# Split-precision chunked scan and expert layer: the first sweep's second product in fp32 from unsplit operands, and a first tile with masked logs

## The chip, the cores and the metric

One core of one Trainium2 chip runs the whole program. The metric is the device time of one execution in microseconds (us). In the profile PE is the matrix engine TensorE (PEld is its weight load), DVE is VectorE, ACT is ScalarE, POOL is GpSimd and SP is SyncE, which issues the DMAs.

## The reference

Two stages follow each other. The first is a scan with decay over 4 batches, 8 heads and 768 positions, head size 32 and state size 16; the second is a dense layer 256 to 2048 to 256 with `h - tanh(h)` between its two products.

```
log_a = log(clip(a, 1e-6, 1))
for each chunk:
    cum = cumsum(log_a in the chunk)
    L = exp(cum[i] - cum[j]) for i >= j, else 0
    y_intra = ((C @ B.T) * L) @ x
    y_inter = (C @ state) * exp(cum)
    state = exp(cum[-1]) * state + sum_j B[j] x[j] exp(cum[-1] - cum[j])
h = y @ w_in
g = h - tanh(h)
out = g @ w_out
```

## The kernel before

Tokens lie along the free axis, features along the partitions. The scan is done in 28 chunks of up to 112 positions (`Q = 112`, 7 chunks per batch); a state of 16 rows is carried in front of each chunk, so that a chunk has 128 rows. The dense layer works on 8 tiles of tokens, four of 256 tokens and four of 512 (`WIDTH`). The first four tiles are swept together: each of four sweeps takes four of the 16 blocks of the hidden layer (`SWEEPS`) through those four tiles, so that the weights, which arrive from memory meanwhile, are needed piece by piece. The last four tiles each take all 16 blocks at once.

Both products of the dense layer are done in split precision. A number is stored as a high and a low part in the type fp32r, and a product is three matmuls (high by high, high by low, low by high). So the weights are converted when they arrive (`conv`, L290 to L337: ACT and DVE rebuild fp32 from the 64-bit words in `raw`, ACT casts the high part `wh` at L321, DVE subtracts for the low part `wl` at L324), the scan's output is split into `xh` (ACT, L569) and `xl` (DVE, L572), and the hidden layer into `gh` (ACT, L651) and `gl` (DVE, L657). `mm1` (L629) is the first product, into `ph`; `act` applies tanh on ACT (L643) and subtracts on DVE (L647), into `g`; `mm2` (L683) is the second product, into `o`. In the narrow tiles one step of `mm1` or `mm2` covers two blocks of the hidden layer: 12 products of 128x128 by 128x256.

A chunk of the scan runs as a chain over the engines. For the first tile (chunks 0 to 2, `first_tile`, L378) PE forms the running sums of the logs in two halves of four heads each (`cp`, fp32, L387), ACT takes exp of one head at a time with a bias (`lt`, L404), PE forms C by B (`att`, L397), DVE multiplies (L409), POOL sets what lies above the diagonal to zero (L414), and PE multiplies by x (`y`, L541). For chunks 3 to 9 (`chunk_a`, L438) the difference of the sums comes out of one bf16 matmul of 9 rows (L451, from `lt_c` and `rt_c`, small tables that are sent through device memory as `cum3`), ACT does one exp of all heads (L460), DVE the product (L464), POOL the mask (L476). From chunk 10 on (`chunk_l`, L479) the sums arrive broadcast by a DMA from `cumr`. Chunk 10 is the first whose state is carried within the 128 rows: its `y` at L541 has the shape 128x128, once in the first sweep, and serves below as a mark in the trace. `z` (L553) is the state for the next chunk in chunks 0 to 4, in a place of its own; ACT copies it into the next `x` (L566).

The order of all instructions is made ahead of the run by a list scheduler in the program (`Order`, L52 to L218). Each operation is handed over with its engine and a cost in us; the scheduler tries 16 rounds of priorities from a random seed and keeps the best by its own costs. The engines then run their instructions strictly in that order, each with its semaphore waits. So any change of a cost, a table or the seed moves instructions on all engines.

## Time and profile before

| what | value |
|---|---|
| median of 3 runs | 337.64 us (335.47 to 447.55) |
| the profiled execution | 337.02 us |
| its span, first to last instruction | 335.1 us |
| PE busy | 321.2 us, 96% of the span |
| PE weight load | 269.7 us, 80% |
| DVE busy | 226.3 us, 68% |
| ACT busy | 218.3 us, 65% |
| POOL busy | 57.0 us, 17% |
| moved by DMA | 32.16 MB, mean 96 GB/s |

The time of the profiled execution is 1.9 us longer than its span: that part lies before the first and behind the last instruction. Busy shares are means over stages that differ; the stage that the change touches is the first fifth of the span. A matmul in fp32 is recorded as two instructions, one in fp32r or bf16 as one.

### The profile page before, as it was taken

The page shows a single profiled execution, that of the slowest core. Times are in us where ns is not written, and L with a number is a line of the kernel's source. Part 1 is how long each engine was busy: PE and PEld are TensorE (multiplying, and loading weights), DVE is VectorE, ACT ScalarE, POOL GpSimd, SP SyncE. Part 2 cuts the span into 40 slices and gives each one's busy share as a digit, 9 for nine tenths or more (in the row PEclk, how much of TensorE's full clock was granted, in tenths as well). Part 3 has the DMA queues.
Part 4 walks back from the last instruction along what each step waited for, and adds up shares of the span by engine and source line. Part 5 has one row for each costly group of instructions (what it writes and reads, how often), then busy time and mean ns, then how long its engine had stood idle before and what let it go on. Part 6 is the DMA issues. An engine that isn't in the chain of part 4 may idle for free.

```text
span 335.1 us, 6403 instructions
## 1 busy us (share of the span) xinstructions
PE 321.2 (96%) x2452; PEld 269.7 (80%) x2452; DVE 226.3 (68%) x346; ACT 218.3 (65%) x524; POOL 57.0 (17%) x77
## 2 busy tenths in 40 slices
PE   8867989899999999999999999999999999999995
PEld 7656878899999999877877777877787778888884
DVE  5898999999888855764556656456655554545552
ACT  7868889797666635856778783676676664544441
POOL 7445463121000200301111101121011010000000
PEclk9967999999999999999999999999999999999999
DMA  7759885280000006622432033323010000100001
GB/s 219 233 183 344 234 299 161 88 298 3 0 2 2 1 33 220 209 87 86 139 121 94 32 117 99 121 94 115 13 63 2 1 0 2 63 0 2 0 0 63
DMA packets 14441, 32.16 MB, mean 96 GB/s; under 512 B 2500, under 2 KB 5452, under 8 KB 14412
## 3 DMA queue, kind: packets, MB, share of 16 engines
q1 hardware_dynamic: 14412, 31.77, 28.4%
q8 instruction: 19, 0.31, 0.4%
q14 instruction: 10, 0.08, 0.1%
HBM read 28.33 MB, written 3.43 MB: 95 GB/s over the span
## 4 chain that ended last, share of the span: by engine, by line
PE 82%; DMA 8%; DVE 4%; ACT 2%; SPq 1%; issue 1%; POOL 0%; POOLq 0%
PE o L683 39%; PE ph L629 38%; DMA raw<-w_d 5%; PE y L541 3%; PE att L528 2%; DMA bc<-bc_d 2%; DMA braw<-bn_d 1%; ACT wv L300 1%; ACT lt L404 1%; DVE gl L657 1%; ACT x L566 0%; SPq L871 0%; DVE g L647 0%; DVE wm L305 0%; DVE xl L572 0%
## 5 line engine op out<-in xcount | busy, mean ns | idle before, releaser
L647 DVE TENSOR_TENSOR g<-ph,g 128x512 f32<-128x512 f32 x96 | 66.0, 689 | 67.6 <-ACT g L643 67.4
L643 ACT ACTIVATE g<-ph 128x512 f32<-128x512 f32 x96 | 57.2, 597 | 67.6 <-PE ph L629 65.9
L629 PE MATMUL ph<-xh,wh 128*128 128x256 f32 (+1 forms) x256 | 85.8, 346 | 0.0
L629 PE MATMUL ph<-xh,wl 128*128 128x256 f32 (+1 forms) x256 | 84.6, 341 | 0.0
L657 DVE TENSOR_TENSOR gl<-g,gh 128x512 fp32r<-128x512 f32 x96 | 68.8, 716 | 20.0 <-ACT gh L651 18.9
L651 ACT CAST gh<-g 128x512 fp32r<-128x512 f32 x96 | 59.5, 620 | 26.4 <-DVE g L647 25.4
L683 PE MATMUL o<-gh,wh 128*128 128x256 f32 (+1 forms) x256 | 72.2, 343 | 0.1
L683 PE MATMUL o<-gh,wl 128*128 128x256 f32 (+1 forms) x256 | 71.2, 339 | 0.0
L683 PE MATMUL o<-gl,wh 128*128 128x256 f32 (+1 forms) x256 | 70.8, 338 | 0.0
L629 PE MATMUL ph<-xl,wh 128*128 128x256 f32 (+1 forms) x256 | 65.8, 338 | 0.2 <-DVE xl L572 0.2
L476 POOL TENSOR_SCALAR_AFFINE_SELECT lt<-lt 128x896 f32<-128x896 f32 (+1 forms) x25 | 28.0, 1121 | 202.9 <-ACT lt L494 180.4
L629 PEld LDWEIGHTS ph<-xh,wh 128*128 128x128 f32 x256 | 49.2, 192 | 7.8 <-issue 1.6
L629 PEld LDWEIGHTS ph<-xh,wl 128*128 128x128 f32 x256 | 49.2, 192 | 5.3
L629 PEld LDWEIGHTS ph<-xl,wh 128*128 128x128 f32 x256 | 44.3, 191 | 6.0 <-DVE xl L572 0.4
L683 PEld LDWEIGHTS o<-gh,wh 128*128 128x128 f32 x256 | 41.5, 188 | 7.8 <-issue 1.9
L683 PEld LDWEIGHTS o<-gl,wh 128*128 128x128 f32 x256 | 41.6, 189 | 5.5
L683 PEld LDWEIGHTS o<-gh,wl 128*128 128x128 f32 x256 | 41.4, 188 | 5.2
L494 ACT ACTIVATE lt<-lt,ncum 128x112 f32<-128x112 f32 (+1 forms) x144 | 41.9, 377 | 0.0
L541 PE MATMUL y<-lt,x 128*32 128x128 f32 (+2 forms) x448 | 18.0, 275 | 6.4 <-ACT wh L321 3.1
L541 PEld LDWEIGHTS y<-lt,x 128*32 128x32 f32 x448 | 10.7, 110 | 14.0 <-issue 6.1
L532 DVE TENSOR_TENSOR lt<-att,lt 128x896 f32<-128x896 f32 (+1 forms) x18 | 19.0, 1058 | 0.0
L564 ACT COPY x<-s 16x64 f32<-16x64 f32 x60 | 14.4, 241 | 1.4 <-DVE s L559 0.7
(79 smaller groups left out, 229.8 us busy)
## 6 DMA issues: line engine op xcount, KB each, us to landing
lt<-cumr SPq DMA_DIRECT2D x18, 512.0 KB
raw<-w_d SPq DMA_DIRECT2D x16, 512.0 KB
bc<-bc_d SPq DMA_DIRECT2D x14, 352.0 KB
x<-x_d SPq DMA_DIRECT2D x14, 256.0 KB
out_d<-ob SPq DMA_DIRECT2D x8, 256.0 KB
braw<-bn_d SPq DMA_DIRECT2D x14, 112.0 KB
out_d<-ob SPq DMA_DIRECT2D x8, 128.0 KB
cum<-parts SPq DMA_DIRECT2D x1, 168.0 KB
```

What stands on the lines that cost most here:

```text
L476: nc.gpsimd.affine_select(out=k["l"][:, :, 0:q], in_=k["l"][:, :, 0:q], pattern=[[0, H], [1, q]], compare_op=ALU.is_ge, fill=0.0, base=N, ...
L494: nc.scalar.activation(k["l"][:, h, 0:q], k["l"][:, h, 0:q], AF.Exp, bias=ncum[:, h, ck : ck + 1])
L528: nc.tensor.matmul(out=a_[:, i], lhsT=bb[r], rhs=cc[r, :, 0 : qlen(ck + 1 + j)], start=True, stop=True)
L532: nc.vector.tensor_tensor(out=l, in0=chs[j]["a"], in1=l, op=ALU.mult)
L541: nc.tensor.matmul(out=y[r, hg * P : hg * P + P] if both else v[r, hg], lhsT=d["x"][:, cg, P * hg + D * h : P * hg + D * h + D], rhs=k["wh ...
L564: nc.scalar.copy(to.rearrange("p (g h d) -> p g h d", g=2, h=4)[:, :, i], k["s"][D * i : D * i + N])
L629: nc.tensor.matmul(out=ph[:, i * w : i * w + w], lhsT=w_[:, u, 0, k, j * P : (j + 1) * P], rhs=(xh, xl)[p][:, k, ts], start=p == 0 and k = ...
L643: nc.scalar.activation(g, gs[t, f][0], AF.Tanh)
L647: nc.vector.tensor_tensor(out=g, in0=ph, in1=g, op=ALU.subtract)
L651: nc.scalar.copy(gh, gs[t, f][1])
L657: nc.vector.tensor_tensor(out=gl, in0=g, in1=gh.bitcast(F32), op=ALU.subtract)
L683: nc.tensor.matmul(out=po[t, seg][e], lhsT=w_[:, u, 1, j, e * P : (e + 1) * P], rhs=g[:, i * w : i * w + w], start=f == seg[0] and k == 0 ...
```

## The change

Three parts, and with them a new order.

1. In the first sweep (tiles 0 to 3, blocks 0 to 3 of the hidden layer, eight steps of `mm2`) the second product takes `g` and the weights `wf` as they are, in fp32: four matmuls per step in the place of twelve. For these steps the parts `gh` and `gl` are not made. The output weights of the first two 512-row pieces are rebuilt into `wf`, and their split into `wh` and `wl` (`parted`) is moved behind, to just before tile 4 needs it. The second piece is converted in halves, as the first.
2. In the first tile POOL masks the logs ahead of the sums (`fn_k`), so that PE's sums come out as differences; PE adds a large negative number above the diagonal with one more bf16 matmul (`eye` by `never`), and ACT does one exp of 448 columns per half where it did four of 112. The mask behind the product is gone.
3. The fill of `rt_c` (`signs`) moves from POOL to DVE, the layout of `cum3` changes so that four loads of `rt_c` replace eight, and `cum3` is written by two DMAs where it was one. The scheduler's rate of DMA, its look-ahead, its seed and some costs are other numbers.

```diff
+NEVER = -2.0 ** 15
...
-APART, URGE = 5, 3.0
+APART, URGE, WHOLE = 5, 3.0, 2
...
-    DMA_LATENCY, SEM, SEM_PE, RATE, FLIGHT = 0.8, 0.15, 0.28, 0.24e6, 8
-    ROUNDS, JITTER, SEED, EARLY, LOOK = 16, 0.3, 69, 5.0, 0.35
+    DMA_LATENCY, SEM, SEM_PE, RATE, FLIGHT = 0.8, 0.15, 0.28, 0.32e6, 8
+    ROUNDS, JITTER, SEED, EARLY, LOOK = 16, 0.3, 174, 5.0, 0.5
...
+        def whole(s):
+            return u < WHOLE and s.start == 1
...
-            nc.vector.scalar_tensor_tensor(out=wv[u][:, s], in0=wv[u][:, s], scalar=0x80000000, in1=wm[u][:, s],
+            to = wv[u][:, s]
+            if whole(s):
+                to = wf[:, u : u + 1].bitcast(U32)
+            nc.vector.scalar_tensor_tensor(out=to, in0=wv[u][:, s], scalar=0x80000000, in1=wm[u][:, s],
                                            op0=ALU.bitwise_and, op1=ALU.bitwise_or)
...
+            if whole(s):
+                op("DVE", 1.2 * k, lambda s=s: fn4(s), r=[n_m[i], n_v[i]], w=[f"wf{u}"])
+                continue
...
+    def parted(u, after):
+
+        w_ = wf[:, u].rearrange("p (k c) -> p k c", k=2)
+        op("ACT", 0.62, lambda: nc.scalar.copy(wh[:, u, 1], w_), r=[f"wf{u}"], w=[f"wh{u}.1"], after=after)
+        op("DVE", 0.7, lambda: nc.vector.tensor_tensor(out=wl[:, u, 1], in0=w_, in1=wh[:, u, 1].bitcast(F32), op=ALU.subtract),
+           r=[f"wf{u}", f"wh{u}.1"], w=[f"wl{u}.1"])
...
+        def fn_k(ck, i):
+            chs[ck]["k", i] = p3.tile([P, BANK], F32, tag="g", name=f"lm{ck}_{i}").rearrange("p (h m) -> p h m", h=4)
+            nc.gpsimd.affine_select(out=chs[ck]["k", i], in_=la[:, 4 * i : 4 * i + 4, ck : ck + 1].broadcast_to([P, 4, P]),
+                                    pattern=[[0, 4], [-1, P]], compare_op=ALU.is_gt, fill=0.0, base=0, channel_multiplier=1)
+
         def fn_f(ck, i):
             f = chs[ck]["f", i] = ps_h.tile([P, 4, P], F32, tag="ph", name=f"cp{ck}_{i}")
+            nc.tensor.matmul(out=f[:, :, 0:Q], lhsT=eye, rhs=never.unsqueeze(1).broadcast_to([P, 4, Q]),
+                             start=True, stop=False, skip_group_check=True)
             for h in range(4):
-                nc.tensor.matmul(out=f[:, h, 0:Q], lhsT=la[:, 4 * i + h, ck : ck + 1].broadcast_to([P, P]),
-                                 rhs=upto[:, N:P], start=True, stop=True)
+                nc.tensor.matmul(out=f[:, h, 0:Q], lhsT=chs[ck]["k", i][:, h], rhs=upto[:, N:P], start=False, stop=h == 3,
+                                 skip_group_check=True)
...
-            for h in range(4):
-                nc.scalar.activation(chs[ck]["l"][:, 4 * i + h, :], chs[ck]["f", i][:, h, 0:Q], AF.Exp,
-                                     bias=ncum[:, 4 * i + h, ck : ck + 1])
+            nc.scalar.activation(chs[ck]["l"][:, 4 * i : 4 * i + 4], chs[ck]["f", i][:, :, 0:Q], AF.Exp)
...
-        def fn_s(ck, i):
-            lt = chs[ck]["l"][:, 4 * i : 4 * i + 4]
-            nc.gpsimd.affine_select(out=lt, in_=lt, pattern=[[0, 4], [1, Q]], compare_op=ALU.is_ge,
-                                    fill=0.0, base=N, channel_multiplier=-1)
...
-                n_f = slot("ph", NPH)
-                op("PE", 1.2, lambda ck=ck, i=i: fn_f(ck, i), r=["la", "upto"], w=[n_f])
-                op("ACT", 1.05, lambda ck=ck, i=i: fn_x(ck, i), r=[n_f, "ncum", "tab"], w=[k["n_l"][i]], urge=URGE)
+                n_f, n_k = slot("ph", NPH), slot("g", 3)
+                op("POOL", 0.7, lambda ck=ck, i=i: fn_k(ck, i), r=["la"], w=[n_k], urge=URGE)
+                op("PE", 1.2, lambda ck=ck, i=i: fn_f(ck, i), r=[n_k, "upto", "never"], w=[n_f])
+                op("ACT", 0.52, lambda ck=ck, i=i: fn_x(ck, i), r=[n_f, "tab"], w=[k["n_l"][i]], urge=URGE)
                 if i == 0:
                     op("PE", 0.55, lambda ck=ck: fn_p(ck), r=[grp[ck // CPG]["n_bc"]], w=[n_a[ck % 2]])
                 op("DVE", 0.6, lambda ck=ck, i=i: fn_m(ck, i), r=[n_a[ck % 2]], w=[k["n_l"][i]], urge=URGE)
-                op("POOL", 0.8, lambda ck=ck, i=i: fn_s(ck, i), w=[k["n_l"][i]], urge=URGE)
...
+    def native(t, f):
+        return t < NSW and f // 2 < WHOLE
...
+        if native(t, f):
+            gs[t, f, 0] += [n_g]
+        else:
+            n_gh, n_gl = slot("gh", 3), slot("gl", 3)
+            gs[t, f, 0] += [n_gh, n_gl]
 
         def fn_t():
             g = p3.tile([P, BANK], F32, tag="g", name=f"g{t}_{f}")
...
 
         op("ACT", 0.6, fn_t, r=[n_h], w=[n_g])
         op("DVE", 0.69, fn_s, r=[n_h], w=[n_g])
+        if native(t, f):
+            return
...
+            if native(t, f):
+                for i in range(blocks(t)):
+                    for e in range(2):
+                        u, j = divmod(f + i, 2)
+                        nc.tensor.matmul(out=po[t, seg][e], lhsT=wf[:, u, 256 * j + e * P : 256 * j + (e + 1) * P],
+                                         rhs=gs[t, f][1][:, i * w : i * w + w], start=f == seg[0] and i == 0 and e == 0,
+                                         stop=last and i == blocks(t) - 1, skip_group_check=True)
+                return
+            _, _, gh, gl = gs[t, f]
...
-        op("PE", 12 * rate(w) * blocks(t), fn, r=[n_h, n_l, f"wh{f // 2}.1", f"wl{f // 2}.1"], w=n_po[t, seg])
+        if native(t, f):
+            op("PE", 16 * rate(w) * blocks(t), fn, r=[*n_in, f"wf{f // 2}"], w=n_po[t, seg])
+        else:
+            op("PE", 12 * rate(w) * blocks(t), fn, r=[*n_in, f"wh{f // 2}.1", f"wl{f // 2}.1"], w=n_po[t, seg])
...
+    def masks():
+        nc.gpsimd.memset(eye, 1.0)
+        nc.gpsimd.affine_select(out=eye, in_=eye, pattern=[[-1, P]], compare_op=ALU.is_equal, fill=0.0, base=0,
+                                channel_multiplier=1)
+        nc.gpsimd.memset(never, 0.0)
+        nc.gpsimd.affine_select(out=never, in_=never, pattern=[[1, Q]], compare_op=ALU.is_ge, fill=NEVER, base=N,
+                                channel_multiplier=-1)
...
-        nc.gpsimd.tensor_scalar(out=v, in0=nc.const_aps.tensor(1.0, (P, 1), F32).broadcast_to(v.shape),
+        nc.vector.tensor_scalar(out=v, in0=nc.const_aps.tensor(1.0, (P, 1), F32).broadcast_to(v.shape),
...
-    def put_parts():
-        nc.sync.dma_start(out=cum3.rearrange("j p q m -> q (j p) m"),
-                          in_=parts[0:HR].rearrange("q j p m -> q (j p) m"))
+    def put_parts(j):
+        nc.sync.dma_start(out=cum3[:, 4 * j : 4 * j + 4].rearrange("p h c m -> (h c) p m"), in_=parts[0:HR, j])
...
-            for w in range(2):
-                nc.sync.dma_start(out=rt_c[32 * i : 32 * i + 3, w], in_=src[:, w, :, N:P])
+            nc.sync.dma_start(out=rt_c[32 * i : 32 * i + 3].rearrange("r w c m -> r w (c m)"), in_=src)
...
-    conv(1)
+    conv(1, True)
...
+    for u in range(WHOLE):
+        plan(begin["t", NSW] - 6 + 2 * u, lambda u=u: parted(u, [len(op.ops) - 1]))
```

What the order of the instructions makes of it, at three places.

On DVE, at the start of the weights' conversion and the first tile's multiplications by `att` (`lt` are the three chunks' decay tables, `wm` and `wv` the weights of the first piece, half by half, `raw` as they arrive). Before:

```order
L305 TENSOR_SCALAR wm_192<-raw_139 128x512
L409 TENSOR_TENSOR lt_173<-att_178,lt_173 128x4x112 x2
L310 TENSOR_SCALAR wv_201<-wv_201 128x512
L313 SCALAR_TENSOR_TENSOR wm_192<-wv_201,wm_192 128x512
L317 SCALAR_TENSOR_TENSOR wv_201<-wv_201,wm_192 128x512
L409 TENSOR_TENSOR lt_214<-att_178,lt_214 128x4x112 x2
```

and now:

```order
L310 TENSOR_SCALAR wm_202<-raw_152 128x512
L315 TENSOR_SCALAR wv_198<-wv_198 128x512
L318 SCALAR_TENSOR_TENSOR wm_202<-wv_198,wm_202 128x512
L325 SCALAR_TENSOR_TENSOR wv_198<-wv_198,wm_202 128x512
L310 TENSOR_SCALAR wm_202<-raw_152 128x512
L315 TENSOR_SCALAR wv_198<-wv_198 128x512
L432 TENSOR_TENSOR lt_183<-att_234,lt_183 128x4x112 x2
L432 TENSOR_TENSOR lt_228<-att_234,lt_228 128x4x112 x2
L318 SCALAR_TENSOR_TENSOR wm_202<-wv_198,wm_202 128x512
L588 TENSOR_TENSOR xl<-y_269,xh 128x2x112
L325 SCALAR_TENSOR_TENSOR wf<-wv_198,wm_202 128x512
L432 TENSOR_TENSOR lt_267<-att_234,lt_267 128x4x112 x2
```

The first chunk's two multiplications stood behind one step of the conversion and now stand behind six.

On POOL, in the same stretch (`lm` are the masked logs, `la` the logs, `bw` the decayed B). Before:

```order
L806 TENSOR_SCALAR rt_c<-const-float32-1.0,par 128x784 x2
L357 COPY bc_126<-idn 128x2x16
L414 AFFINE_SELECT lt_173<-lt_173 128x4x112 x2
L350 TENSOR_TENSOR bw_226<-braw_94,wdec 128x256
L357 COPY bc_161<-idn 128x2x16
L414 AFFINE_SELECT lt_214<-lt_214 128x4x112 x2
```

and now:

```order
L404 AFFINE_SELECT lm_0_157<-la 128x512
L404 AFFINE_SELECT lm_1_163<-la 128x512
L404 AFFINE_SELECT lm_0_172<-la 128x512
L375 COPY bc_129<-idn 128x2x16
L404 AFFINE_SELECT lm_1_185<-la 128x512
L368 TENSOR_TENSOR bw_200<-braw_97,wdec 128x256
L404 AFFINE_SELECT lm_0_215<-la 128x512
```

The fill of `rt_c` has left POOL, and its six selects stand ahead of PE's sums instead of behind DVE's products.

On PE, at the second product of the second tile in the first sweep (`o` is its accumulator, `y` a chunk's output). Before:

```order
L541 MATMUL y_756<-lt_671,x_586 32x112 x8
L553 MATMUL y_756<-x_586,bw_673 16x32 x8
L683 MATMUL o_0_0_776<-gh_0_636,wh 128x256 x4
L683 MATMUL o_0_0_776<-gh_0_636,wl 128x256 x4
L683 MATMUL o_0_0_776<-gl_0_668,wh 128x256 x4
L683 MATMUL o_0_0_776<-gh_2_695,wh 128x256 x4
```

and now:

```order
L706 MATMUL o_0_0_641<-g_0_608,wf 128x256 x4
L557 MATMUL y_657<-lt_589,x_496 32x112 x8
L569 MATMUL y_657<-x_496,bw_535 16x32 x8
L706 MATMUL o_0_0_641<-g_2_625,wf 128x256 x4
L467 LDWEIGHTS lt_c
```

Twelve matmuls of a step have become four, each of them two instructions in the profile, and they read `g` and `wf`.

## Rows read from the trace of the kernel before

**Rows 1.** the page: DVE busy and PE clock, tenths, 40 slices of 8.4 us
```profile
DVE  5898999999888855764556656456655554545552
...
PEclk9967999999999999999999999999999999999999
```

**Rows 2.** stretches: us, busy (count) by engine, PEclk, DMA share, GB/s
```profile
20.18:61.39 41.21, 35.53 (x497) 30.58 (x494) 39.55 (x49) 32.74 (x75) 20.20 (x18) 0.90 0.79 261
61.39:331.30 269.91, 269.91 (x1784) 226.53 (x1784) 170.45 (x260) 169.48 (x404) 25.14 (x38) 1.00 0.19 63
```

**Rows 3.** timeline of PE: start, us, engine, line, operation [idle before, releaser]
```profile
25.04 0.38 PE L451 MATMUL att<-rt_c,lt_c 9*128 9x224 bf16 x4 [0.47 <-DVE lt L464]
...
30.96 0.59 PE L541 MATMUL y<-lt,x 128*32 128x112 f32 x16 [0.64 <-POOL bc L357]
...
32.78 0.26 PE L451 MATMUL att<-rt_c,lt_c 9*128 9x192 bf16 x4 [1.12 <-DVE lt L464]
...
37.57 0.28 PE L451 MATMUL att<-rt_c,lt_c 9*128 9x224 bf16 x4 [0.41 <-DVE lt L464]
...
43.86 0.59 PE L541 MATMUL y<-lt,x 128*32 128x112 f32 x16 [1.49 <-DVE xl L572]
...
56.08 0.50 PE L629 MATMUL ph<-xl,wh 128*128 128x256 f32 x2 [0.23 <-DVE xl L572]
...
61.39 0.65 PE L541 MATMUL y<-lt,x 128*32 128x128 f32 x16 [1.26 <-issue]
```

**Rows 4.** groups by line and shape, first 62 us: busy, mean | idle
```profile
L657 DVE TENSOR_TENSOR gl<-g,gh 128x512 fp32r<-128x512 f32 x7 | 6.3, 896 | 0.1
L460 ACT ACTIVATE lt<-att 128x896 f32<-128x896 f32 x6 | 5.5, 921 | 1.4 <-PE att L456 1.1
L324 DVE TENSOR_TENSOR wl<-wv,wh 128x1024 fp32r<-128x1024 f32 x3 | 3.6, 1208 | 0.0
```

**Rows 5.** stretches around the fall of the clock, columns as rows 2
```profile
17.00:18.00 1.00, 0.00 (x0) 0.00 (x0) 1.00 (x3) 1.00 (x3) 0.34 (x1) 1.00 0.06 16
...
27.00:28.00 1.00, 1.00 (x6) 1.00 (x6) 0.65 (x1) 0.99 (x4) 0.00 (x0) 0.50 0.98 349
...
29.00:30.00 1.00, 1.00 (x30) 0.68 (x28) 0.17 (x2) 0.74 (x2) 1.00 (x2) 1.00 1.06 341
```

**Rows 6.** timeline of PE, fp32 products of the first 14 us
```profile
5.19 0.54 PE L845 MATMUL pr<-la,upto 128*128 128x224 f32 x2
...
8.51 1.93 PE L387 MATMUL cp<-upto,la 128*128 128x112 f32 x16
...
12.06 1.14 PE L387 MATMUL cp<-upto,la 128*128 128x112 f32 x8
```

**Rows 7.** chain that ended last: one block of the second product
```profile
58.70 1.42 PE o L683 x12
```

**Rows 8.** timeline of the first tile, all engines
```profile
5.77 0.39 DVE L876 TENSOR_SCALAR ncum<-pr 128x224 f32<-128x224 f32 x1 [2.00 <-PE pr L845]
...
9.34 0.43 DVE L305 TENSOR_SCALAR wm<-raw 128x512 uint32<-128x512 uint32 x1 [1.26 <-DMA raw<-w_d]
...
9.68 1.15 DVE L409 TENSOR_TENSOR lt<-att,lt 128x448 f32<-128x448 f32 x2
...
10.16 2.06 ACT L404 ACTIVATE lt<-cp,ncum 128x112 f32<-128x112 f32 x8
...
10.37 1.30 POOL L414 TENSOR_SCALAR_AFFINE_SELECT lt<-lt 128x448 f32<-128x448 f32 x2 [3.48 <-DVE lt L409]
...
11.27 0.95 DVE L313 SCALAR_TENSOR_TENSOR wm<-wv,wm 128x512 uint32<-128x512 uint32 x1
...
11.47 0.65 PE L541 MATMUL y<-lt,x 128*32 128x112 f32 x16
...
15.64 0.69 DVE L313 SCALAR_TENSOR_TENSOR wm<-wv,wm 128x512 uint32<-128x512 uint32 x1
...
19.28 0.97 PE L541 MATMUL y<-lt,x 128*32 128x112 f32 x16 [3.07 <-ACT wh L321]
```

More of the change, by code (lines that the diff above doesn't have):

```diff
@@ L450, in fn_p @@
                 r = slice(32 * i, 32 * i + 9)
-                nc.tensor.matmul(out=at_[:, i, 0:2, :], lhsT=lt_c[r, ck - NEAR.start], rhs=rt_c[r, :, ck - NEAR.start, 0:q],
+                nc.tensor.matmul(out=at_[:, i, 0:2, :], lhsT=lt_c[r, ck - NEAR.start], rhs=rt_c[r, :, ck - NEAR.start, N : N + q],
                                  start=True, stop=True)
@@ L824, in tile_ssm_moe @@
     op("ACT", 0.9, ones, w=["lt_c"])
+    for w in range(2):
+        op("DVE", 0.85, lambda w=w: signs(w), r=["par"], w=["rt_c"])
     for G in range(2):
```

33 lines of the change are left out of this document (17 added, 16 removed).

## Prediction

> **What bounds the kernel now.** I read the page's slices first. The reader is to see that DVE is at eight tenths or more in every slice from the second to the tenth, 8 to 84 us, and falls to about a half behind them, and that the clock is below full only in the third and fourth slice, 17 to 34 us [rows 1]. So there are two regimes. The second reading, by stretch, cuts them apart: from 61.39 us to 331.30 PE is busy for all of its 269.91 us at full clock, without a gap, while from 20.18 to 61.39, 41.21 us, PE is busy for 35.53 at a mean clock of 0.90, and DVE for 39.55 [rows 2]. The kernel's end therefore moves one for one with the moment at which the gapless part begins, plus or minus what is added to PE behind it. That moment is the product of chunk 10, the first `y` of shape 128x128 [rows 3]. Both orders hand PE the same work ahead of it: eight steps of the first product, six of the eight second products of the first sweep, ten chunks. I price the change on this mark.
>
> The 41.21 us ahead of the mark fall into three parts. PE's gaps are 41.21 - 35.53 = 5.7 us; seven gaps of 0.2 to 1.5 us make 5.6 of them, and five are ended by DVE; POOL ends one, and the last is listed without a releaser [rows 3]. The clock's loss is 0.10 x 41.21 = 4.1 us. The remaining 31.4 us is work at full clock. The largest single reason for the gaps is a DVE that has 39.55 us of work in 41.21: whatever ACT or PE hand it stands in a queue.
>
> **The second product, what it removes.** Ahead of the mark six casts and six subtractions for `gh` and `gl` fall away; the subtraction takes 896 ns in the mean of seven in the first 62 us [rows 4], so DVE is rid of 6 x 0.90 = 5.4 us. The second halves of two weight pieces also lose their low part, half of 1208 ns each [rows 4], 1.2 us, and the order moves one whole such subtraction behind the mark, 1.2 us. That is 7.8 us off DVE; since records on one engine overlap by some hundredths, I count 7.5. If DVE alone set the mark, it would come 7.5 us earlier, at 53.9. ACT is rid of as many casts; it has 8 us of idle in the stretch already [rows 2] and I count nothing for it. The moved splits (`parted`) are two pieces of about 0.6 us on each engine in a part where DVE is busy 170 of 270 us [rows 2]; PE's gapless run hides them, and if it did not, they would cost 1.2 us.
>
> **What it adds.** PE pays. A step in split precision takes 1.42 us [rows 7]. A step in fp32 is four products, each recorded as two instructions over 256 columns. The trace has fp32 with fewer columns: 16 instructions of 112 columns take 1.93 us and 8 take 1.14, so eight more cost 0.79, or 0.099 each, 0.88 ns a column; with the fill it is 0.121 each, 1.08 ns a column; two of 224 columns take 0.54 with the fill [rows 6]. Scaled to 256 columns and eight instructions a step takes 1.8 us by the first figure and 2.2 by the second; if the columns alone counted, and the fixed part not, it would be lower, 1.7. I take 1.83, near to the first, because a step runs back to back with other matmuls. So each step adds 0.41 us (0.3 to 0.8): 6 x 0.41 = 2.5 ahead of the mark and 2 x 0.41 = 0.8 behind it.
>
> The Trainium skill (FP8 and Floating Point Precision, TensorE Precision Notes) says that true fp32 goes through the array in four passes, where the split form makes three products; this is the rule that speaks against the change. An estimate by it, four products of four passes over 256 columns at 2.4 GHz, is 1.71 us a step, and the sum below would be 1 us better with it than with 1.83. No row here shows an fp32 matmul of 256 columns.
>
> **The first tile.** ACT does one exp of 448 columns for each half where it did four heads; eight heads take 2.06 us [rows 8], a half 1.03, and 896 columns in one instruction take 921 ns [rows 4], so a half comes to about 0.5 (0.4 to 0.6), 6 x 0.5 = 3 us less on ACT. POOL's selects, 0.65 us each [rows 8], leave the path between DVE and PE and stand ahead of PE's sums: `la` is ready early, three of six are issued before anything else asks POOL. PE gets six bf16 matmuls of 448 columns; the nearest row is four of 224 columns in 0.28 [rows 3], so 0.14 to 0.6 each, 0.8 to 3.6 in all; I take 1.2, and PE's three idle microseconds in this tile [rows 8] hide it. The fill of `rt_c` on DVE is two instructions of 896 columns; two multiplications with 896 columns between them take 1.15 [rows 8], so two fills take 2.3 at the most, in a place where DVE idles for 2.00 waiting for PE [rows 8]: 0 to 0.3, I take 0. The queue of SP carries four small loads less, and one write more, on the way to the next weights; a DMA ends none of the seven gaps, so I count 0 (half a microsecond either way).
>
> Against this stands the order on DVE. The first chunk's multiplications wait behind six conversion steps instead of one. From 9.34, when the weights land as before, I sum: steps of about 0.4 and 0.95 in turn [rows 8], with half a microsecond for ACT between, bring DVE to 13.3; four multiplications of 0.57 [rows 8] to 15.6; two heavy steps at 0.69 and the low part of chunk 0 to 17.4; the last two multiplications to 18.6. The first `y` then comes at 14.7 instead of 11.47, but the third, which alone feeds what follows, at 19.0 instead of 19.28 [rows 8]. Behind it come the state of that chunk and the first `att` of `chunk_a`, at about 20.0 where it was 20.18. So the first tile gains next to nothing by itself, 0.2 us (-1.5 to +2).
>
> What it changes is the shape of PE's idle. Before, PE does nothing from the end of the second chunk until 19.28, 3.07 us at one stretch [rows 8], and with it the granted clock falls from 1.00 to 0.50, and comes back between 28 and 29 us [rows 5]: 1.2 GHz where it had been 2.4, for some ten microseconds of nearly full work. By the sum above PE's idle is broken up: about 1.5 us near 10 us (a buffer of `ph` waits for an exp), 0.6 near 14 and 1.4 near 18, with work of the sums between. A stretch of 30 to 33 us in which gaps of 0.64 and 1.12 us stand close together [rows 3] did not lower the clock [rows 1, 5]. I take it that the clock stays full: 4.1 us.
>
> The Trainium skill (TensorE: Matmul & The Clock Gate, HAM oscillation — how this bites in real kernels) says the same, that idle stretches between bursts of matmuls put the engine at its lower clock and short ones do not; the trace agrees, with 3.07 us before the fall.
>
> **What is left of the gaps.** With 7.5 us off DVE most of its queue is gone, but not the loop of the chunks: there is one buffer for `att`, so the next `att` waits for the exp and the multiplication before it, 0.92 + 1.0 us and three hand-overs. Walking PE's new order against it I find one gap of 0.9 us near 22 us and several of 0.2 to 0.4. I keep 2.5 of the 5.7 us (0.5 to 5.7).
>
> **The sum.** The mark: 20.0 + 31.4 + 2.5 (fp32) + 2.5 (gaps) = 56.4, where it was 61.39: 5.0 us earlier, and DVE's own 53.9 does not hold it up. Behind it 0.8 is added. 5.0 - 0.8 = 4.2 us. The profiled execution took 337.02 us, its span and the 1.9 around it; 337.0 - 4.2 = 332.8. The median of the runs is 337.64, 0.6 above, within their scatter; I forecast on the profiled one.
>
> **Rivals.**
> *The clock falls all the same* (chance 0.2). For it: the idle of PE between 9 and 20 us is hardly less in total, 3.5 us, and the later first `y` may join two gaps. Against it: the stretch at 30 us. It costs the 4.1 us: 336.9, no difference.
> *The gaps stay* (0.12). The loop of `att` and not DVE's queue is the limit, fed by ACT; for it, POOL's and the unlisted gap; against it, that five of seven are ended by DVE. 5.7 instead of 2.5: 336.0.
> *The gaps all but go* (0.14). 0.5 instead of 2.5, with the lower price of fp32, 0.3: 330.1 to 330.8.
> *Slower: the first tile comes late* (0.09). Place: POOL's selects and DVE's conversions at 5 to 13 us. The heavy conversion step took 0.95 us beside a POOL select and 0.69 without one [rows 8]; if POOL is held up as much as DVE, the masked logs come late, PE waits for POOL where it never did, the first `y` at 14.7 slips by two or three more, and the third with it. PE then idles 3 us or more at a stretch and the clock falls earlier. Price: 3.3 for the tile and 3.3 in all for the eight fp32 steps, with the clock's loss and the gaps as they were: 337.0 + 3.3 + 3.3 = 343.6; with half of the tile's delay and half of the gaps gone, 337.0 + 1.7 + 3.3 - 2.9 = 339.1. It decides from the point where the third `y` comes later than 21 us.
> *The change does not act*: if the first sweep's end were set by DMA, nothing would come earlier and the fp32 price would be added, 337.0 + 3.3 = 340.3; 0.02, since a DMA ends none of the gaps.
>
> **How the numbers follow.** The forecast holds 0.43, 331 to 335 by its own bounds (the fp32 price and the start of the tile). Down to the case without gaps and up past the clock's case I reach 330.6 to 338.0, which leaves out the slow case and half of the fastest, 0.17. Two per cent of the time before is 6.7 us, about what a measurement of this kernel can tell from no change. Faster by more needs under 330.3, part of the case without gaps: 0.08. Slower by more needs 343.8, the worst end of the late tile: 0.03. The rest, 0.89, is within.
>
> **What would show it.** In the profile of the changed kernel: the 128x128 `y` at 56.4 (55 to 58); no slice with a clock under full; a step of L706 at 1.7 to 1.9 us; DVE busy about 7.5 us less up to the mark and idle in it, waiting for ACT; the third `y` of the first tile near 19 us; PE without a gap from the mark to the end. It is wrong if the clock falls near 15 to 20 us, if PE's first sums wait for POOL for long, or if gaps on PE before the mark are still over 5 us and ended by ACT's exp.

## The result and the profile after the change

| what | before | after |
|---|---|---|
| median of 8 runs each, one chip | 337.31 us | 334.25 us (333.12 to 334.84) |
| ratio, with its 95% interval | | 0.9916 [0.9893, 0.994] |
| the profiled execution | 337.02 us | 333.12 us |
| its span | 335.1 us | 331.1 us |
| PE, DVE, ACT, POOL busy | 321.2, 226.3, 218.3, 57.0 us | 320.8, 223.2, 210.1, 52.9 us |

The kernel is 0.8% faster (0.6 to 1.1%): 3.1 us by the medians, 3.9 by the two profiled executions, where 4.2 were forecast. The profiled execution after, 333.12 us, is the fastest of its eight; the other seven took 334.14 to 334.84. The predicted 332.8 us lies 1.45 below the median, and the median lies within the forecast range. One of the eight runs before took 447.55 us; the ratio is taken without such slow runs.

DVE's and PE's slices on the page of the kernel after, as [rows 1]:

```profile
DVE  7889999998797857755666555755565464645451
...
PEclk9999999999999999999999999999999999999999
```

The clock is full in every slice; in eight runs its mean was 0.998 to 1.0. DVE is at nine tenths from the fourth to the ninth slice, 25 to 75 us. The stretches of the kernel after, as [rows 2], with the columns given there, and third the stretch from the landing of the first weights to the mark:

```profile
19.11:56.23 37.12, 34.35 (x460) 27.69 (x453) 35.34 (x46) 29.47 (x70) 17.60 (x17) 1.00 0.85 286
56.23:327.40 271.17, 270.99 (x1776) 225.47 (x1776) 171.99 (x262) 168.48 (x403) 26.94 (x38) 1.00 0.20 65
9.87:56.23 46.36, 41.39 (x599) 33.53 (x599) 44.08 (x63) 36.40 (x89) 18.79 (x20) 1.00 0.78 260
```

The mark came at 56.23, 5.16 us earlier. On PE's side: the first `att` is 1.07 earlier (19.11 for 20.18), the gaps are 37.12 - 34.35 = 2.8 where they were 5.7, no clock is lost (4.1 less), and the work at full clock is 34.35 where it was put at 31.4: 1.07 + 2.9 + 4.1 - 2.95 = 5.1. Behind the mark PE is gapless as before (the 0.18 us without work lie behind its last matmul); that part grew by 1.1 us.

Its waits on PE, in the timeline of the kernel after, as [rows 3]:

```profile
11.03 0.35 PE L409 MATMUL cp<-never,eye 128*128 128x448 bf16 x1 [1.78 <-ACT lt L428]
...
18.47 0.59 PE L557 MATMUL y<-lt,x 128*32 128x112 f32 x16 [1.04 <-ACT x L582]
...
22.32 0.28 PE L467 MATMUL att<-rt_c,lt_c 9*128 9x224 bf16 x4 [0.55 <-DVE lt L480]
...
23.63 0.31 PE L569 MATMUL z<-x,bw 128*16 128x32 f32 x16 [0.54 <-POOL bw L368]
...
50.51 1.99 PE L706 MATMUL o<-g,wf 128*128 128x256 f32 x8 [0.19 <-DVE g L670]
...
56.23 0.65 PE L557 MATMUL y<-lt,x 128*32 128x128 f32 x16 [0.90 <-issue]
```

The third `y` is at 18.47, and the two long gaps of the first tile are the ones that the prediction put near 10 and 18 us. And the waits on DVE, from the same timeline:

```profile
9.87 0.43 DVE L310 TENSOR_SCALAR wm<-raw 128x512 uint32<-128x512 uint32 x1 [1.02 <-DMA raw<-w_d]
...
24.77 0.47 DVE L310 TENSOR_SCALAR wm<-raw 128x512 uint32<-128x512 uint32 x1 [0.65 <-DMA raw<-w_d]
...
37.60 0.69 DVE L670 TENSOR_TENSOR g<-ph,g 128x512 f32<-128x512 f32 x1 [0.44 <-ACT g L666]
```

The second row is new: VectorE waits for the second half of the second weight piece. In the chain that ended last that transfer is a link (columns: start, us, what):

```profile
19.21 5.54 DMA raw<-w_d
```

There is a second way to add up the same 5.16 us, on VectorE alone. From the landing of the first weights to the mark it was busy for 50.25 us of 52.05 (9.34 to 61.39, the kernel before) and is busy for 44.08 of 46.36 (9.87 to 56.23): 6.17 less work, 0.48 more idle, 0.53 later landing, 5.16 in all. The same stretch in the kernel before:

```profile
9.34:61.39 52.05, 42.86 (x615) 36.03 (x615) 50.25 (x67) 42.34 (x107) 25.83 (x26) 0.90 0.73 240
```

Both sums close, as they must, since each only splits one stretch into its parts. So they do not say whether PE's clock and gaps or VectorE's queue set the mark. The timeline of VectorE says one thing more. The mark reads the product of chunk 10 that VectorE makes, before and after:

```profile
59.61 1.08 DVE L532 TENSOR_TENSOR lt<-att,lt 128x896 f32<-128x896 f32 x1
```

```profile
54.46 1.08 DVE L548 TENSOR_TENSOR lt<-att,lt 128x896 f32<-128x896 f32 x1
```

The mark starts 1.78 us behind the start of that step before, 1.77 after, and 1.77 to 1.85 behind it in 13 of the 14 profiles of this study. (The exception, 3.93, is the kernel with two sweeps in fp32, where PE has no gap ahead of the mark.) In both profiles the step follows another one on VectorE without a wait. What sets it is the question for the experiments.

### The profile page after: what moved, and what is told of

Same layout as the page of the kernel before. It is cut to its first block, busy times and chain, and to the rows that moved or that the text cites. A ratio compares the mean times of both kernels' runs of the same rounds, so it can differ in the third digit from the quotient of the medians.

```text
span 331.1 us, 6326 instructions
## 1 busy us (share of the span) xinstructions
PE 320.8 (97%) x2426; PEld 266.2 (80%) x2426; DVE 223.2 (67%) x345; ACT 210.1 (63%) x500; POOL 52.9 (16%) x79
## 4 chain that ended last, share of the span: by engine, by line
PE 88%; DMA 4%; DVE 3%; SPq 2%; ACT 1%; issue 1%; ACTq 0%
PE ph L646 39%; PE o L716 38%; DMA raw<-w_d 4%; PE y L557 4%; PE o L706 3%; PE att L544 2%; DVE wm L318 1%; SPq L913 1%; DVE lt L480 1%; SPq L915 1%; PE att L472 1%; DVE wv L325 0%; ACT lt L428 0%; ACT lt L476 0%; PE cp L412 0%
## 5 line engine op out<-in xcount | busy, mean ns | idle before, releaser
L646 PE MATMUL ph<-xh,wh 128*128 128x256 f32 (+1 forms) x256 | 84.4, 341 | 0.0
L680 DVE TENSOR_TENSOR gl<-g,gh 128x512 fp32r<-128x512 f32 x88 | 62.2, 707 | 23.8 <-ACT gh L674 22.3
L674 ACT CAST gh<-g 128x512 fp32r<-128x512 f32 x88 | 54.5, 619 | 26.8 <-DVE g L670 25.7
L716 PE MATMUL o<-gh,wh 128*128 128x512 f32 (+1 forms) x224 | 67.5, 353 | 0.0
L716 PE MATMUL o<-gl,wh 128*128 128x512 f32 (+1 forms) x224 | 65.7, 345 | 0.0
L716 PE MATMUL o<-gh,wl 128*128 128x512 f32 (+1 forms) x224 | 65.6, 345 | 0.0
L716 PEld LDWEIGHTS o<-gh,wh 128*128 128x128 f32 x224 | 36.9, 188 | 8.5 <-issue 2.8
L716 PEld LDWEIGHTS o<-gl,wh 128*128 128x128 f32 x224 | 36.9, 188 | 5.9
L716 PEld LDWEIGHTS o<-gh,wl 128*128 128x128 f32 x224 | 36.9, 188 | 5.3
L706 PE MATMUL o<-g,wf 128*128 128x256 f32 x64 | 15.8, 390 | 0.2 <-DVE g L670 0.2
```

The costliest lines, as they stand in the source:

```text
L646: nc.tensor.matmul(out=ph[:, i * w : i * w + w], lhsT=w_[:, u, 0, k, j * P : (j + 1) * P], rhs=(xh, xl)[p][:, k, ts], start=p == 0 and k = ...
L674: nc.scalar.copy(gh, gs[t, f][1])
L680: nc.vector.tensor_tensor(out=gl, in0=g, in1=gh.bitcast(F32), op=ALU.subtract)
L706: nc.tensor.matmul(out=po[t, seg][e], lhsT=wf[:, u, 256 * j + e * P : 256 * j + (e + 1) * P], rhs=gs[t, f][1][:, i * w : i * w + w], start ...
L716: nc.tensor.matmul(out=po[t, seg][e], lhsT=w_[:, u, 1, j, e * P : (e + 1) * P], rhs=g[:, i * w : i * w + w], start=f == seg[0] and k == 0 ...
```

## The experiments

All were timed beside the kernel before on the same chip (medians there 336.4 to 336.7 us); clocks are means over a run.

**The product alone.** The kernel before with part 1 of the change (`native`, `wf`, `parted`, the second piece in halves), the old first tile and the old scheduler's numbers:

```diff
+    def native(t, f):
+        return t < NSW and f // 2 < WHOLE
...
-    conv(1)
+    conv(1, True)
```

> The kernel before with the second product of the first sweep in fp32 alone: the old first tile, the old numbers of the scheduler. Theory A (the two halves need each other: the first tile's shape keeps the clock, the fp32 product empties the queue of VectorE): the clock falls to 1.2 GHz near 18 us as before and costs about 4 us, so of 4 us little is left, time within 1 us of 337, the mark (first 128x128 y) at 60 to 61 us. Rival B (the relief of VectorE brings it all): the mark near 57, time 333 to 334. Rival C (the new order alone): 336 to 338.

Measured: 335.69 us, ratio 0.9969 [0.9947, 0.9991]; clock 0.982 to 0.988 in all runs; mark at 60.35 in the profiled run, which is the slowest of the twelve (336.74 us). VectorE has room (34.78 us busy in 41.95), the clock falls all the same, and 0.7 us remain. The mark is where theory A put it (60 to 61):

```profile
18.40:60.35 41.95, 37.82 (x468) 30.42 (x466) 34.78 (x47) 28.34 (x69) 16.30 (x18) 0.88 0.71 236
```

Ahead of the mark it is not VectorE's queue that comes last here. The step that the mark reads waits for POOL's mask, which stands behind eight exps on ACT (2.34 us from 55.08):

```profile
58.51 1.09 DVE L549 TENSOR_TENSOR lt<-att,lt 128x896 f32<-128x896 f32 x1 [1.64 <-POOL lt L493]
```

**The first tile alone.** The changed kernel with the second product split as before:

```diff
-            return u < WHOLE and s.start == 1
+            return False
...
-        return t < NSW and f // 2 < WHOLE
+        return False
...
-    conv(1, True)
+    conv(1)
...
```

> The changed kernel with the second product of the first sweep split as before: the new first tile and the new numbers of the scheduler stay. Theory A: the clock stays full, which gives up to 4 us to TensorE, but VectorE keeps its 39 us of work ahead of the mark and sets it, so the mark comes at 58.5 to 60 us and the time is 335 to 336. Rival D (the clock is the whole gain): 333. Rival B: 337.

Measured: 343.15 us, 1.0172 [1.0132, 1.0213], mark at 66.92. No theory expected that. The scheduler drew an order in which the first tile is late, the rival that the prediction priced at 339 to 344:

```profile
13.15 1.13 PE L421 MATMUL att<-bc 32*128 32x224 f32 x8 [2.17 <-DVE lt L431]
21.61 0.59 PE L556 MATMUL y<-lt,x 128*32 128x112 f32 x16 [1.05 <-ACT x L581]
25.10 0.39 PE L645 MATMUL ph<-xh,wl 128*128 128x256 f32 x1 [1.99 <-DVE wl L331]
...
37.70 0.35 PE L466 MATMUL att<-rt_c,lt_c 9*128 9x192 bf16 x4 [2.70 <-DVE lt L479]
```

The third `y` is at 21.61, behind the 21 us named as the point from which it decides. The run says little about the tile itself, since the order is another. What the first tile is worth by itself stays open.

**The numbers alone, and all but the numbers.** The scheduler's numbers in the kernel before, and the old ones in the kernel after:

```diff
-    DMA_LATENCY, SEM, SEM_PE, RATE, FLIGHT = 0.8, 0.15, 0.28, 0.24e6, 8
-    ROUNDS, JITTER, SEED, EARLY, LOOK = 16, 0.3, 69, 5.0, 0.35
+    DMA_LATENCY, SEM, SEM_PE, RATE, FLIGHT = 0.8, 0.15, 0.28, 0.32e6, 8
+    ROUNDS, JITTER, SEED, EARLY, LOOK = 16, 0.3, 174, 5.0, 0.5
```

> The kernel before with nothing but the scheduler's rate of DMA, look-ahead and seed of the changed one, so another order of the same work. Theories A, B and D: 336 to 339, the clock falling as before. Rival C (the order is the gain): 333 to 335.

> The whole change under the numbers that the scheduler had before (rate of DMA, seed, look-ahead). With them the fp32 product alone took 335.7 us. Theory A (product and first tile help by what they take off the engines, the numbers choose among orders that differ by 1 to 3 us): 333.5 to 336, and the clock full or not according to where this order puts PE's idle. Rival B (the new numbers are needed for the gain): 337 or more. Rival C (the numbers don't matter): 333.2 to 334.2 with a mark at 56 to 57.

Measured: 338.64 us, 1.0061 [1.0035, 1.0087], mark at 63.86, for the new numbers in the old kernel; 336.00 us, 0.9978 [0.9959, 0.9997], mark at 59.49 and clock 0.988 to 0.995, for the old numbers in the new one. The numbers are no gain of their own (they cost 2 us where nothing else is changed), but of the change's 3 us under its own numbers only 0.7 are left under the old ones, no more than the product alone gave. So part of the gain is the order that the scheduler drew. Each set of numbers has one seed, so how far other seeds would scatter is not shown.

**The clock held in the old kernel.** Twelve idle fp32 matmuls of 64 columns in PE's longest idle stretch, behind the second chunk:

```diff
+            if ck == 1:
+                one = nc.const_aps.tensor(1.0, (P, P), F32)
+                for _ in range(FILL):
+                    nc.tensor.matmul(out=chs[2]["f", 0][:, :, Q:P], lhsT=one, rhs=one[:, 0:64],
+                                     start=True, stop=True, skip_group_check=True)
```

> The kernel before in its own order, with 12 idle fp32 matmuls of 64 columns behind the state of the second chunk, where TensorE stood idle from 16.2 to 19.25 us; what they write is read by nothing. If the idle stretch is what lowers the clock, the granted clock is 1.00 in every slice. Theory A: VectorE, full from 20 to 61 us with under 2 us of idle, then sets the mark, which comes 1 to 2 us earlier only, time 335.5 to 336.5. Rival D: 4 us earlier, 333. If the clock falls all the same, the stretch is not the reason, and the time is 337.

Measured: 337.30 us, 1.002 [0.9994, 1.0045]. The clock was 0.983 to 1.0 (median 0.99; the kernel before there 0.977 to 0.995), so it was raised rather than held; the one run at 1.0 took 336.25 us. In the profiled run, the fastest of the twelve (335.85 us, clock 0.995), the clock is at 1.00 from 20 to 30 us, where it had been at half, and at 0.50 only from 31 to 34 us; the mark is 1.2 earlier, at 60.18. By the mean clock of the stretch 2.5 us are won (0.04 of 40.00 us lost where it was 0.10 of 41.21), but PE's busy time falls by 1.5 only (34.01 for 35.53) and its gaps grow by 0.3. VectorE is busy for 38.86 of 40.00 us, and the step that the mark reads follows in its queue without a wait:

```profile
20.18:60.18 40.00, 34.01 (x489) 29.07 (x489) 38.86 (x48) 32.14 (x74) 20.29 (x18) 0.96 0.80 267
```

So the idle matmuls buy nothing as long as VectorE's queue is that full. That does not make the clock worthless there. The kernel before ran 86 times beside the experiments, on four chips: the 37 runs at a mean clock of 0.985 have a median of 336.9 us, the 13 at 0.995 one of 335.7, the five at 0.98 one of 338.6. A hundredth of the clock is 3.35 us of a time of 335; 1.2 of them show between 0.985 and 0.995.

**Product and held clock together.** The product alone with the same idle matmuls, behind the second chunk's `y`:

> The kernel before with the fp32 second product alone, and twelve idle matmuls (fp32, 64 columns, into an unused column strip of the sums' buffer) behind the second chunk's output, where PE had its longest idle stretch. Without them this kernel took 335.7 us, its clock in the stretch 18.4 to 60.35 us was 0.88, and VectorE was busy for 34.8 of its 42 us. Theory A (the clock and a VectorE with room are worth something only together): the clock stays above 0.97 in the stretch, the mark comes 3 to 5 us earlier, at 55.5 to 57.5, and the time is 331.5 to 333.5. Rival B (the held clock buys nothing here either, as in the old kernel with idle matmuls, because the loop of the chunks sets the mark): clock up, mark 59.5 to 60.5, time 335 to 336.5. Rival C (twelve idle matmuls don't hold the clock here): clock 0.85 to 0.92 as without, 335.7.

Measured: 335.75 us, 0.9961 [0.9939, 0.9984]. The idle matmuls moved the fall of the clock from 20 to 24 us but did not prevent it (stretches of this kernel, columns as [rows 2]):

```profile
23.00:24.00 1.00, 0.00 (x1) 0.02 (x1) 0.81 (x1) 1.00 (x4) 0.00 (x0) 0.98 1.03 368
24.00:25.00 1.00, 0.67 (x12) 0.53 (x11) 0.97 (x3) 0.65 (x4) 0.73 (x1) 0.50 1.06 405
```

The mean clock was 0.987 to 0.994 in eleven of twelve runs (334.6 to 336.7 us); the twelfth, at 1.0, took 332.6 us. So rival C came, and theory A was not put to the test. One run is a hint that the two are worth 3 us together in this order, no proof. In the profiled run (334.59 us) the mark is at 58.24, and the step that it reads waits 1.63 us for POOL's mask, as in the product alone.

**The second sweep in fp32 too.** The price of fp32 where PE has no gap to hide it:

```diff
-APART, URGE, WHOLE = 5, 3.0, 2
+APART, URGE, WHOLE = 5, 3.0, 4
...
-        plan(begin["u", u] - 3, conv, u)
+        plan(begin["u", u] - 3, conv, u, u < WHOLE)
```

> The changed kernel with fp32 second products in the second sweep too, eight more steps, where PE runs without a gap and VectorE has room. Theory A (a step costs 0.30 us more than a split one, 1.72 for 1.42, and no relief of VectorE is worth anything behind the mark): the stretch from the mark to the last matmul grows by 8 x 0.30 = 2.4 us, 271.0 to 273.4; with the mark unmoved the time is 2.4 us above the changed kernel's. Rival B (the price of the forecast, 0.41): 3.3 us. Rival C (relief of VectorE and ScalarE helps everywhere, through fewer waits or less contention): 0 to 1 us. The scheduler draws another order, so the mark may move by 1 or 2 us by itself; the stretch behind it tells the theories apart.

Measured: 338.31 us, 1.0035 [1.0015, 1.0055], 4.6 us above the changed kernel. The mark is 0.67 later than in the changed kernel beside it, and the clock was 0.988 to 0.995, which leaves the stretch behind the mark as the measure. From the mark at 57.70 the last matmul starts 273.62 us later, in the changed kernel beside it 270.59 us: 3.03 for eight steps, 0.38 each. That is nearer to the forecast's 0.41 than to the 0.30 that one step shows (below), and no gain from the relief of VectorE shows there.

**The changed kernel again, and its first tile ahead.** The second one has the same schedule, but the first chunk's `att`, two exps and two multiplications stand ahead of the first weights' conversion:

```diff
-        start = best[1]
-        for i in sorted(range(n), key=lambda i: (start[i], i)):
+        start, d = best[1], self.id
+        self.moves = [(d["f", 1, 0], [d["p", 0]]), (d["wv"] + 2, [d["x", 0, 1], d["x", 1, 0], d["wv"], d["m", 0, 0], d["m", 0, 1], d["wv"] + 1])]
...
```

> The changed kernel once more, as the measure for the others on this chip. All theories: ratio 0.988 to 0.995 against the kernel before, clock at 0.998 or above, mark near 56.2.

> The changed kernel with the same schedule but for the first tile: the first C-by-B product goes ahead of the third sum on PE, the next two exps go ahead of the first conversion of weights on ScalarE, and the first chunk's two multiplications go ahead of it on VectorE, which idles for 1.02 us there until the weights land at 9.87. Theory A (from the weights' landing to the mark VectorE's queue sets the pace, so 1.0 us of its work done ahead of the landing brings all that follows forward): PE's gap of 1.78 us near 11 is gone, third output 0.8 to 1.1 earlier, at 17.4 to 17.7, mark near 55.2, time 0.7 to 1.1 us under the changed kernel's. Rival B (the loop of PE, ScalarE and VectorE through the chunks sets the pace): the gap goes, another opens behind it, mark 55.9 to 56.5, time within 0.3 us. Rival C (PE's idle, moved, lets the clock fall): clock under 0.99, time 1 to 3 us above.

Measured: 333.74 us, 0.9906 [0.9879, 0.9933], for the changed kernel; 333.71 us, 0.9912 [0.9888, 0.9937], with the tile ahead. In that one the third `y` came at 17.51 instead of 18.31, and the clock then fell:

```profile
16.00:17.00 1.00, 0.06 (x9) 0.00 (x0) 1.00 (x3) 0.95 (x5) 0.00 (x0) 1.00 0.04 9
17.00:18.00 1.00, 0.49 (x12) 0.52 (x16) 1.00 (x4) 0.37 (x2) 0.00 (x0) 0.79 0.04 14
18.00:19.00 1.00, 1.00 (x31) 0.74 (x23) 0.78 (x4) 0.46 (x3) 0.00 (x0) 0.50 0.52 70
...
25.48:56.89 31.41, 29.97 (x383) 24.34 (x383) 30.48 (x38) 24.75 (x58) 15.13 (x14) 1.00 0.82 275
```

and none of it mattered: the mark is at 56.89 with half the clock from 18 to 24 us, and at 57.03 in the changed kernel beside it with the clock full. The profiled run, at 0.990, took 333.40 us, and two runs with the tile ahead, at 0.999 and 1.0, took 333.6. What the two share is a step of VectorE, first the one with the tile ahead, then the changed kernel:

```profile
25.48 0.43 DVE L322 TENSOR_SCALAR wm<-raw 128x512 uint32<-128x512 uint32 x1 [0.32 <-DMA raw<-w_d]
```

```profile
25.62 0.43 DVE L310 TENSOR_SCALAR wm<-raw 128x512 uint32<-128x512 uint32 x1 [1.43 <-DMA raw<-w_d]
```

The mark comes 31.41 us behind it in both, and 31.46 in the first profile (24.77 to 56.23). Whatever is gained ahead of that landing is lost in the wait for it. The equal distance alone does not tell VectorE's queue from the loop of the chunks, since the three profiles share the order from that step on; the last experiment does.

**The landing earlier.** The half piece is issued at 19.21 us, behind eight small loads that keep SP from 12.73 to 17.82 and three other DMAs, while the DMA engines have little to do (a stretch of the kernel after; 37 GB/s):

```profile
15.40:19.40 4.00, 2.96 (x88) 2.37 (x90) 4.00 (x10) 3.13 (x12) 0.00 (x0) 1.00 0.18 37
```

One edit puts it ahead of them, where it is issued near 11 us; a second kernel has both edits:

```diff
...
+        order = sorted(range(n), key=lambda i: (start[i], i))
+        order.remove(d["raw", 1, 1])
+        order.insert(order.index(d["parts", 0, 0]), d["raw", 1, 1])
...
```

> The changed kernel with one DMA issued earlier on SP: the second half of the second weight piece, which stood behind the eight small loads of lt_c and rt_c (issued at 19.21 us, while the DMA engines were nearly idle from 15.4 to 19.5), stands ahead of them. In three profiles of the changed schedule VectorE waits for that landing, 0.65, 1.43 and 0.32 us, at 24.77, 25.62 and 25.48, and the mark follows the landing by 31.46, 31.41 and 31.41 us, whether the first tile was early or late and whether the clock had been full before or not. Theory A (that landing sets the mark): VectorE's wait there goes, the mark comes 0.6 to 1.4 us earlier, near 55.4, the time is 0.6 to 1.4 us under the changed kernel's. Rival B (the wait is slack, the loop of the chunks sets the mark): within 0.3 us of the changed kernel. Rival C (the small loads come late behind 512 KB): the first att of the later chunks waits for rt_c by 0.5 us or more, and the time is 0.5 to 1.5 us above the changed kernel's.

> Both edits at once: the first tile's steps ahead of the weights' conversion (which made the third output 0.8 us earlier and the time no shorter), and the half piece of weights loaded ahead of the small loads. Theory A (the landing near 25 us hid what the earlier first tile had gained): both gains show, mark 54.5 to 55.3, time 1.4 to 2.2 us under the changed kernel's, 331.5 to 332.3 where that takes 333.7. Rival B (the loop sets the mark): as with one edit, 333.4 to 333.9. Rival C (with PE's idle put together near 16 us the clock falls from 17 to 25 us and the gain is spent on that): clock 0.99, time 332.8 to 334.

Measured: 332.82 us, 0.9886 [0.9856, 0.9915], with the landing earlier, 333.94 us, 0.9905 [0.988, 0.993], with both. With the landing earlier alone VectorE no longer waits there, and the mark follows the same step by 31.40 us:

```profile
24.51 0.42 DVE L314 TENSOR_SCALAR wm<-raw 128x512 uint32<-128x512 uint32 x1
```

```profile
55.91 0.65 PE L561 MATMUL y<-lt,x 128*32 128x128 f32 x16 [0.94 <-issue]
```

It is the fastest kernel of the study: 0.9 us under the changed kernel by the medians, as theory A expected, and 0.7 by the ratios to the kernel before, the fairer measure, since the two ran on different chips. The intervals overlap, so by the times alone the gain is not shown. Five of its six runs took 332.70 to 333.19 us at a clock of 0.998 or more; the sixth, at 0.990, took 335.08. Both edits together lose it again: the earlier tile now meets `rt_c` and `bw` that are not there yet,

```profile
19.45 0.25 PE L481 MATMUL att<-rt_c,lt_c 9*128 9x224 bf16 x1 [0.54 <-DMA rt_c<-cum]
...
24.62 0.31 PE L583 MATMUL z<-x,bw 128*16 128x32 f32 x16 [1.56 <-POOL bw L382]
```

and behind the second wait the clock falls to 0.50 (26 to 28 us); the clock was 0.990 to 0.995 in all six runs. The mark is at 57.63. Rival C's clock and time came (0.99, 332.8 to 334), but in another place; none of the three theories had this wait.

**More work on VectorE.** The kernel with the early landing and three idle multiplications more on VectorE (they land near 36 us, not near 29 as the expectation says):

```diff
+            if ck == 5:
+                for _ in range(MORE):
+                    nc.vector.tensor_scalar(out=spare, in0=spare, scalar1=1.0, scalar2=None, op0=ALU.mult)
```

> The kernel with the half piece of weights loaded early (332.8 us, mark 55.91, full clock, no wait of VectorE for a landing behind 10 us) and three idle multiplications of 128x512 on VectorE more, about 1.2 to 1.3 us of its time, behind the low part of chunk 5's output near 29 us; they read and write a tile that nothing else uses. Theory A (from about 25 us on VectorE's queue sets the mark: in four profiles the mark comes 31.4 us behind one of its steps, and in the stretch it is idle for less than 1 us): the mark comes 1.0 to 1.3 us later, at 56.9 to 57.2, the time is 333.8 to 334.1. Rival B (PE and the loop of the chunks set the mark, VectorE's share is cover): mark within 0.4 us of 55.9, time 332.6 to 333.2.

Measured: 334.67 us, 0.9942 [0.9917, 0.9968], 1.9 above by the medians and by the ratios (another chip again), more than theory A's 1.0 to 1.3. Part of that is the clock: the four of twelve runs at 0.997 or more took 333.42 to 334.59, 0.9 above the five such runs of the kernel without the extra work (332.70 to 333.19) by the medians, and the two at 0.989 and 0.990 that were slowest took 335.90 and 336.90. In the profiled run the clock was 0.999:

```profile
35.99 1.34 DVE L596 TENSOR_SCALAR spare<-spare 128x512 f32<-128x512 f32 x3
```

```profile
57.48 0.65 PE L561 MATMUL y<-lt,x 128*32 128x128 f32 x16 [0.94 <-issue]
```

The mark is 1.57 later. Part of that was there before the idle work: VectorE's last `xl` ahead of it starts at 35.69 where it did at 35.03. From that step to the mark are 21.79 us instead of 20.88, so 0.91 of 1.34 us arrive. VectorE's wait of 0.25 us near 37, which is gone here, took up some of the rest. That is just under theory A's answer (1.0 to 1.3), and far from rival B's, at 0.4. It rests on one profile of each kernel.

## Why the prediction came out, step by step

**Where to look** was right: the time follows the mark, and PE is all but gapless behind it in every kernel of the study (0.11 us at most). One reading of the slices was not: DVE stays at eight tenths up to the fourteenth slice, 117 us, and not to 84.

**The mark at 56.4** was right as a number (56.23), and its terms nearly so: the start at 20.0 (19.11 measured, 0.9 better), fp32 and work at 31.4 + 2.5 (34.35, 0.45 worse), the gaps at 2.5 (2.8). That 0.9 and 0.7 cancel is luck. Of the work 6 x 0.30 to 6 x 0.38, 1.8 to 2.3 us, is fp32. The other 0.7 to 1.1 was there before: worked out in the same way, the old kernel with the idle matmuls has 34.01 - 0.04 x 40.00 = 32.4 us of work at full clock. So 31.4 was about 1 too low, and the clock's 4.1, taken from the same 41.21, about 1 too high.

**"DVE's own 53.9 does not hold it up"** is the step that failed. In the kernel after, VectorE does set the mark. It was rid of 6.17 us and not of 7.5, the first weights landed 0.53 later, and it idled 0.48 more: its own sum gives 56.23. That PE's sum came to 56.4 as well is in part luck.

The terms that were counted are there. Group of DVE by line and shape, first 9.34 to 61.39 us before, then 9.87 to 56.23 after, columns as [rows 4]; the last line is from the timeline after:

```profile
L657 DVE TENSOR_TENSOR gl<-g,gh 128x512 fp32r<-128x512 f32 x6 | 5.6, 930 | 0.0
...
L324 DVE TENSOR_TENSOR wl<-wv,wh 128x512 fp32r<-128x512 f32 x2 | 1.4, 687 | 0.0
```

```profile
L332 DVE TENSOR_TENSOR wl<-wv,wh 128x1024 fp32r<-128x1024 f32 x2 | 2.4, 1208 | 0.0
...
L332 DVE TENSOR_TENSOR wl<-wv,wh 128x512 fp32r<-128x512 f32 x2 | 1.7, 874 | 0.0
```

```profile
56.05 1.21 DVE L332 TENSOR_TENSOR wl<-wv,wh 128x1024 fp32r<-128x1024 f32 x1
```

The subtractions for `gl` took 5.58 us (5.4 counted). Of `wl` with 1024 elements there were three ahead of the mark [rows 4]; one became a half, and one now starts at 56.05, behind the step that the mark reads. Inside the stretch `wl` takes 1.87 us less (2.4 counted). What was not counted is two other things. The heavy conversion steps (L313 and L317, now L318 and L325) take 15.29 us where they took 14.67. Two of the six `gl` had lasted 1.39 and 1.47 us beside a select on POOL, the other four 0.67 to 0.69; now two conversion steps of 128x1024 last 1.78 and 1.82 beside a select, where the third takes 1.23. So part of the 0.90 us per `gl` lay in POOL's selects, which now meet other steps. And neighbouring records overlap by 3.2 us in all where they did by 4.1; 0.3 had been allowed for that.

The mark lies 31.4 us behind one VectorE step in four profiles, with that step at 24.51, 24.77, 25.48 and 25.62. Where the step waits for the weights' landing it moves with it (two profiles of the changed kernel: landing 0.85 later, mark 0.80 later, time 0.81 longer); where the landing is early, VectorE's own queue sets it, at 24.51. Of work added to VectorE seven tenths reach the mark, in one profile. The equal distance is not the whole of VectorE's account: ACT holds it up once on the way, by 0.44 us near 37 (0.25 with the early landing). In the product alone, with VectorE at 34.78 of 41.95 us, ACT's exps and POOL's mask come last instead. How the 3 us divide among product, tile and order is not shown.

**"A DMA ends none of the seven gaps, so I count 0"** failed with it. It was read on PE's waits in the kernel before. After the change VectorE's queue is short enough to meet the next landing and waits there, 0.65 and 1.43 us in two profiles of the changed kernel. The queue of SP was priced as a cost to transfers, not as what would be late next.

**The clock, 4.1 us.** It stays full, as forecast, and PE's sum needs about 3 us of it (above). But what it is worth depends on what else is waited for. Lost for six microseconds ahead of the landing, with the tile ahead, it cost nothing. With the early landing one run at 0.990 took about 2 us more than the five at 0.998 or more, and with more work on VectorE the runs at 0.989 and 0.990 took 2 to 3 us more than those at 0.997 or more. In the old kernel the step from 0.985 to 0.995 goes with 1.2 us. PE and VectorE were two limits close together, and the change moved both. The rival *the clock falls all the same* shows in the product alone, 335.7 (336.9 priced). The Trainium skill (TensorE: Matmul & The Clock Gate, HAM oscillation — how this bites in real kernels) says that short idle stretches leave the clock up and derives the loss from the time spent at the lower level. The trace differs on the first, since with the tile ahead the clock fell behind an idle stretch of 1.45 us; on the second it differs in that kernel alone, where the time at 1.2 GHz cost nothing, since TensorE was not the only limit.

**A step of fp32, 1.83 us.** Timeline of the kernel after:

```profile
61.45 1.89 PE L706 MATMUL o<-g,wf 128*128 128x256 f32 x8
62.98 0.47 PE L646 MATMUL ph<-xh,wh 128*128 128x256 f32 x1
```

The next product starts 1.53 us on and takes 0.47, 0.19 longer than such a matmul does elsewhere in the profile (0.28): 1.72 for the step, 0.30 over the split one. The Trainium skill (FP8 and Floating Point Precision, TensorE Precision Notes) led to an estimate of 1.71, which this step meets. The step right behind the mark, read in the same way, takes 1.64 + 0.19 = 1.83:

```profile
56.81 1.99 PE L706 MATMUL o<-g,wf 128*128 128x256 f32 x8
58.45 0.47 PE L646 MATMUL ph<-xh,wh 128*128 128x256 f32 x1
```

It stands behind a chunk's `y` and not behind a wide product, so the neighbours count. Eight steps in a gapless stretch cost 0.38 each, 1.80 a step, so for a sum the forecast's 1.83 was the better number.

**0.8 behind the mark** became 1.1, of which two steps explain 0.6 to 0.8; the rest is open.

**The first tile.** The third `y` at 18.47 (19.0 forecast), the exps 0.54 each (0.5), the fill of `rt_c` ahead of the first weights (3.38 to 4.65). Those landed 0.53 later in the profile. *Gaps stay* and *the change does not act* did not occur. *The first tile comes late* did, in the tile alone.

## What to carry to other kernels

Where two engines are both nearly full ahead of the point that sets the end, add up the change on each of them, and take the later; a gain on one alone (a fuller clock, a shorter queue) is worth less than its own sum until the other moves. When a queue gets shorter, ask which landing it will meet, and look whether that transfer stands behind small ones in the issuing queue while the DMA engines idle. Where a scheduler draws the order, part of a change's worth is the draw: run the parts under either set of numbers before giving the gain to a part.
